# Raw sums of x kept in DRAM, and the down weights' GpSimd work dealt out by units

## The chip, the cores and the metric

The kernel runs on one core of one Trainium2 chip. The metric is device time in microseconds from start to end of one execution, lower is better. Where several executions of a kernel were timed, their median stands for it.

The engines are named as the profile names them: PE is TensorE (matmuls), PEld its weight loads, DVE is VectorE, ACT is ScalarE, POOL is GpSimd, SP is SyncE, which here only issues DMA. Every engine runs its own instructions in program order and waits for the others by semaphores. A DMA that an engine issues waits in that engine's order too, so an issue that cannot go yet holds everything that is queued behind it on this engine.

## The reference

For one sequence of S = 2048 tokens of width D = 576, all in float32:

```python
g = sigmoid((x * gate_w).sum(-1, keepdims=True))
a = linear_attention(x, wqkv, wo)      # 32 heads of 18; phi(t) = max(t, 0) + exp(min(t, 0)) + 1e-6
b = (gelu(x @ w_gate) * (x @ w_up)) @ w_down     # inner width 4608
out = g * a + (1 - g) * b
```

The attention is linear: per head a matrix of phi(k) and v and a sum of phi(k) are made over all tokens, and each query's row is multiplied by the matrix and divided by its product with the sum.

## The kernel before

**Split operands.** PE multiplies numbers of a reduced float32 type. Each operand is therefore split into a high part (an ACT or POOL copy into that type) and a low part (raw minus high, on DVE or POOL), and a product is high times high, plus high times low, plus low times high. The contraction of 576 rows is halved into 288 and 288 and each half kept as three row tiles (kt = 0, 1, 2); the third has 32 rows and carries its low part inside the same tile, so a slot of x has five parts: three high, two low.

**Fast 2x2 products.** The three feed-forward products are computed on 2x2 blocks with seven instead of eight block products (`SEQUENCE`, `PRODUCTS`, lines 32 to 35). Their operands are the blocks A11, A12, A22 of x and the sums S1 to S4 of blocks, and for the weights B11, B21, B22 and T1 to T4. The order of the seven is written out by hand.

**Stages in time.** Tokens come in four blocks of 512, which form two pairs (p = 0, 1) for the feed-forward.

1. Keys, gate and the state sums (to about 145 us in the profile).
2. Queries, denominators and the mix (about 145 to 317 us): for each block `query` makes phi(q) in five head groups (lines 420 to 431), `halves_of` splits it on ACT and DVE (`hl`, lines 557 and 558), `den` makes the denominators on PE (line 567). `reciprocals` (lines 626 to 643) inverts them on DVE in two halves per block (line 632), and spreads each to all head rows by a store to DRAM (line 633, `rden_d`) and a load from it (line 637, `rb`), both on SP. `scaled` multiplies phi(q) by it on DVE (line 649) and splits the result into `p` (ACT line 65, DVE line 66). `mixed` multiplies p by the output matrix on PE (line 668) and ACT stores the gated result (line 673). The order of all these calls is written out by hand (lines 688 to 784).
   In the same stage the sums S1 to S4 of the *second* pair's x are made ahead. They come in six pieces (three row tiles, two column halves): `ahead_load` on SP (line 387), `ahead_make` on POOL (four sums by `sum_blocks`, lines 377 to 380, then four casts, line 395, and four subtracts, line 398), and `ahead_store` on SP (lines 405 and 406) of the high and low parts to DRAM (`xop_d`). `next_ahead(k)` stores piece k-1, loads piece k+1 and makes piece k. Two buffers hold pieces, one holds high parts. The first pair's sums come from whole row tiles (`Chunk`), summed on DVE and split by ACT (line 607) and POOL (line 610). At the end of the stage ACT issues the load of the ready gate weights (line 766) into the place where the pieces stood.
3. Gate and up (about 317 to 1131 us): 72 chains, each seven block products of seven matmuls for one pair p, one block column n and one of gate or up (`CHAINS`, `gu_steps`, matmuls in line 806). Eight PSUM banks turn over between PE and its readers. For gate, DVE combines the products and ACT applies the gelu; for up, DVE combines and multiplies, makes the sums of h and stores h to DRAM by SP (line 837). `w_fetch` and `w_split` (lines 810 to 821) load, sum on POOL and split the next weights. The first chains are all of pair 0: chains 0 to 3 are (p 0, n 0) and (p 0, n 1), chains 4 and 5 (p 1, n 1). So the second pair's seven x slots (`X[1]`, tile `xo2`), loaded from `xop_d` in chains 0 to 3 (`XO2_AT`, line 995), are first used in chain 4. The results of pair 0 lie in the tiles `e0` and `e123`, those of pair 1 in `ES[1]`, four tiles `f0` to `f3`.
4. Down (about 1131 us to the end): six groups s of inner rows, each with two pairs p and seven products k, 84 units (`unit`, matmuls in line 1045, 36 to a unit). `h_load` and `h_make` (lines 969, 974 ACT, 975 DVE) bring back and split h three or more units ahead. DVE adds each product into an accumulator in SBUF (line 1053), which starts from the gated attention result (`acc_load`, line 1022). A bank that a later product adds to must have been read by DVE first. `d_fetch` (line 951) loads a group's four down weight blocks; `d_make` (lines 953 to 961) copies one operand on ACT (line 956), makes its low part on POOL in two halves (line 958) and, after B11, makes T1, T2 and T3 in six POOL halves (line 961), after B21 T4 in two. The next group's fetch goes after unit (p 0, k 4), its first two operands after unit (p 1, k 0), then one to a unit.

Of the kernel before, what the change touches and what calls it, by code (L numbers as in the profile page):

```python
# [8 lines left out]
F32 = mybir.dt.float32  # L9
F32R = mybir.dt.float32r  # L10
AF = mybir.ActivationFunctionType
OP = mybir.AluOpType
# [26 lines left out]
def tile_gated_mix(ctx, tc, xt, xs, xn, wk, wv, wq, wo, wgu, wdn, cst, out):  # L39
# [7 lines left out]
    rden_d = {(b, h): dram.tile([7 * NG, BS // 2], F32, name=f"rden_d{b}{h}") for b in range(NB) for h in range(2)}  # L47
    xop_d = dram.tile([128, 7, 5, BS], F32, name="xop_d")
    ga_d = [dram.tile([128, D], F32, name=f"ga_d{i}") for i in range(NST)]
# [334 lines left out]
    def ahead_load(k):  # L384
        kt, c = k // 2, slice(k % 2 * 256, k % 2 * 256 + 256)
        raw = xup.tile([128, 4, 256], F32, name="xu")
        nc.sync.dma_start(raw, xs[1, kt, :, :, c])
        ahead[k] = [raw]

    def ahead_make(k):  # L390
        kt, (raw,) = k // 2, ahead[k]
        sum_blocks(raw, nc.gpsimd)
        hi = xup.tile([128, 4, 256], F32R, name="xuh", bufs=1)
        for i in range(4):
            nc.gpsimd.tensor_copy(hi[:, i], raw[:, i])
            o = raw[:, i].bitcast(F32R) if kt < 2 else hi[32:64, i]
            p = slice(0, 128) if kt < 2 else slice(32, 64)
            nc.gpsimd.tensor_tensor(o, raw[p, i], f32(hi[p, i]), OP.subtract)
        ahead[k] = [hi, raw]

    def ahead_store(k):
        kt, c = k // 2, slice(k % 2 * 256, k % 2 * 256 + 256)
        hi, lo = ahead.pop(k)
        if kt < 2:
            nc.sync.dma_start(xop_d[:, S2:S1 + 1, 3 + kt, c], lo)
# [186 lines left out]
    aheads = Scope()  # L592
    xup = aheads.pool("xup", bufs=2, side="right")
    for k in range(2):
# [97 lines left out]
    query(0, 0)  # L692
    ahead_make(0)
    query(0, 1)
# [255 lines left out]
    def d_fetch(s):  # L950
        nc.sync.dma_start(draw[:, :4], wdn[ORDER[s]].rearrange("p i g c -> p i (g c)"))

    def d_make(s, k):
        b = PRODUCTS[SEQUENCE[k]][1]
        w, src = wd[(7 * s + k) % 8], draw[:, DAT[b]]
        nc.scalar.activation(w[:, 0], src, AF.Copy)  # L956
        for c in (slice(0, 432), slice(432, 864)):
            nc.gpsimd.tensor_tensor(w[:, 1, c], src[:, c], f32(w[:, 0, c]), OP.subtract)  # L958
        for o, x, y in {B11: ((D11, D12, D11), (DX, D22, D11), (D12, D22, D12)), B21: ((D21, D21, DX),)}.get(b, ()):
            for c in (slice(0, 432), slice(432, 864)):  # L960
                nc.gpsimd.tensor_tensor(draw[:, o, c], draw[:, x, c], draw[:, y, c], OP.subtract)  # L961

# [21 lines left out]
    for c, chain in enumerate(CHAINS):  # L984
        for i, step in enumerate(first_steps if c == 0 else gu_steps(*chain)):
            if c or i >= EARLY:
                step()
            if i == 0 and c in at:
                n, m = at[c]
                w_split(m)  # L990
                if (n, m) != (NF2 - 1, 1):
                    w_fetch(n + m, 1 - m)
            for k in XO2_AT.get((c, i), ()):
                a = PRODUCTS[SEQUENCE[k]][0]
# [143 lines left out]
```

## Time and profile before

| | before |
|---|---|
| median of three executions | 1547.41 us (1545.75 to 1548.58) |
| the profiled execution | 1559.55 us |
| its span, first to last instruction | 1557.8 us |
| PE busy | 1511.2 us, 97% |
| DVE, ACT, POOL busy | 65%, 35%, 47% |
| mean clock granted to PE | 0.986 |
| bytes moved by DMA | 248.19 MB, mean 159 GB/s |

The profiled execution is one run with the hardware profiler on; all stamps and durations come from it, and it is 12.1 us longer than the median. "<-" names what ended an engine's wait, as semaphore events show it. Lines are those of the kernel before. In timelines a row is start, duration, engine, line, operation, output and inputs, count, and in brackets the wait before it; rows of SPq and ACTq are DMA issues. In groups the number after the count is total busy time and mean ns of one, then the idle time before them.

### The profile page before, as it was taken

How to read it: one execution, taken by the hardware profiler on the slowest of the kernel's cores; microseconds unless marked ns; L12 is line 12 of the kernel's file. 1: busy time of each engine (PE TensorE's matmuls, PEld its weight loads, DVE VectorE, ACT ScalarE, POOL GpSimd, SP SyncE). 2: the span in 40 equal slices, each digit the busy share in tenths (PEclk: the TensorE clock that was granted, in tenths of full speed). 3: DMA queues.
4: the chain of work that ended last, by engine and by line, in shares of the span. 5: the costliest groups of instructions: out<-in, count | busy, mean ns of one | idle time of the engine just before them, and what ended most of it. 6: DMA issues, size and time to landing. Idle time of an engine off the chain costs nothing.

```text
span 1557.8 us, 21591 instructions
## 1 busy us (share of the span) xinstructions
PE 1511.2 (97%) x8354; PEld 1333.0 (86%) x8354; DVE 1005.9 (65%) x1314; ACT 539.3 (35%) x703; POOL 735.6 (47%) x560
## 2 busy tenths in 40 slices
PE   8999987999999999999999999999999979999999
PEld 8998876887888888888888888888799979999999
DVE  7886765456655566665556666555776676758675
ACT  6554533432223222222322222232234333534431
POOL 3653468165455445445544544552528050725530
PEclk9999988999999999999999999999999989999999
DMA  7553364684323233322223332223795635556574
GB/s 241 151 166 107 131 216 160 214 307 180 111 95 109 97 134 135 135 104 100 105 99 135 135 135 102 101 102 139 269 331 208 208 121 206 168 179 193 184 218 141
DMA packets 99310, 248.19 MB, mean 159 GB/s; under 512 B 8960, under 2 KB 38296, under 8 KB 96264
## 3 DMA queue, kind: packets, MB, share of 16 engines
q1 hardware_dynamic: 96184, 234.96, 43.7%
q10 hardware_dynamic: 3024, 11.86, 2.1%
q8 instruction: 65, 1.06, 0.3%
q14 instruction: 37, 0.30, 0.1%
HBM read 157.24 MB, written 89.55 MB: 158 GB/s over the span
## 4 chain that ended last, share of the span: by engine, by line
PE 75%; issue 2%; DVE 2%; POOL 1%; ACT 1%; DMA 1%; SPq 0%; ACTq 0%; DVEq 0%
PE bank L806 51%; PE bank L1045 22%; PE pair L668 2%; POOL stage L961 1%; POOL wd L958 0%; DMA acc<-ga_d 0%; ACT xo L974 0%; DVE f L834 0%; DVE acc L1053 0%; DMA ga_d<-ga 0%; DMA xop_d<-xuh 0%; ACT wd L956 0%; DVE u L844 0%; ACT ga L673 0%; POOL xo L958 0%
## 5 line engine op out<-in xcount | busy, mean ns | idle before, releaser
L806 PE MATMUL bank<-xo,wu 128*128 128x512 f32 x1764 | 413.3, 394 | 1.5 <-ACT p L850 1.3
L806 PE MATMUL bank<-xo,wg 128*128 128x512 f32 x1764 | 413.4, 394 | 1.2 <-ACT ga L673 0.8
L806 PEld LDWEIGHTS bank<-xo,wu 128*128 128x128 f32 x1764 | 332.4, 189 | 79.2 <-ACT p L850 1.8
L806 PEld LDWEIGHTS bank<-xo,wg 128*128 128x128 f32 x1764 | 332.2, 189 | 78.5 <-ACT ga L673 1.1
L814 POOL TENSOR_TENSOR stage<-stage 128x384 f32<-128x384 f32 x136 | 159.5, 1192 | 45.7 <-DMA stage<-wgu 43.0
L1053 DVE SCALAR_TENSOR_TENSOR acc<-bank,gate,acc 128x288 f32<-128x288 f32 x288 | 137.0, 509 | 58.5 <-PE bank L1045 51.3
L820 POOL TENSOR_TENSOR wg<-stage,wg 128x768 fp32r<-128x768 f32 (+1 forms) x34 | 72.2, 2125 | 190.1 <-ACT wg L819 188.8
L850 ACT ACTIVATE p<-bank 128x512 f32<-128x512 f32 x72 | 43.0, 597 | 343.9 <-PE bank L806 343.9
L820 POOL TENSOR_TENSOR wu<-stage,wu 128x768 fp32r<-128x768 f32 (+1 forms) x34 | 79.8, 2346 | 146.1 <-ACT wu L819 144.8
L1045 PE MATMUL bank<-xo 128*128 128x288 f32 x1044 | 143.6, 297 | 5.1 <-DVE acc L1053 3.8
L1045 PEld LDWEIGHTS bank<-xo 128*128 128x128 f32 x1044 | 141.0, 190 | 6.1 <-DVE acc L1053 4.3
L958 POOL TENSOR_TENSOR wd<-stage,wd 128x432 fp32r<-128x432 f32 x40 | 61.8, 1570 | 155.2 <-ACT wd L956 155.2
L855 DVE TENSOR_TENSOR u<-bank,p 128x512 f32<-128x512 f32 x72 | 49.5, 687 | 94.8 <-PE bank L806 92.2
L1045 PE MATMUL bank<-wd,xo 128*128 128x288 f32 x792 | 107.7, 297 | 1.2 <-DVE acc L1053 1.2
L1045 PEld LDWEIGHTS bank<-wd,xo 128*128 128x128 f32 x792 | 106.4, 190 | 1.5 <-DVE acc L1053 1.5
L958 POOL TENSOR_TENSOR xo<-stage,xo 128x432 fp32r<-128x432 f32 x44 | 64.2, 1486 | 79.3 <-ACT xo L956 79.2
L841 DVE TENSOR_TENSOR e<-bank,u 128x512 f32<-128x512 f32 x54 | 37.2, 691 | 79.7 <-PE bank L806 76.9
L841 DVE TENSOR_TENSOR f<-bank,u 128x512 f32<-128x512 f32 x54 | 37.2, 691 | 76.1 <-PE bank L806 76.0
L831 ACT ACTIVATE f<-f 128x512 f32<-128x512 f32 x54 | 34.1, 632 | 140.8 <-DVE f L841 140.8
L668 PE MATMUL pair<-kw,p 126*128 126x288 f32 (+1 forms) x480 | 71.7, 311 | 9.8 <-ACT p L65 9.7
L668 PEld LDWEIGHTS pair<-kw,p 126*128 126x128 f32 (+1 forms) x480 | 70.9, 204 | 11.6 <-ACT p L65 10.2
L869 DVE TENSOR_TENSOR u<-bank,u 128x512 f32<-128x512 f32 x72 | 49.8, 692 | 38.4 <-PE bank L806 36.4
(189 smaller groups left out, 2314.7 us busy)
## 6 DMA issues: line engine op xcount, KB each, us to landing
h_d<-sx SPq DMA_DIRECT2D x108, 256.0 KB
stage<-wgu SPq DMA_DIRECT2D x34, 768.0 KB
xo<-h_d SPq DMA_DIRECT2D x29, 768.0 KB
e<-h_d SPq DMA_DIRECT2D x28, 768.0 KB
hraw<-h_d SPq DMA_DIRECT2D x27, 768.0 KB
h_d<-e SPq DMA_DIRECT2D x72, 256.0 KB
h_d<-f SPq DMA_DIRECT2D x72, 256.0 KB
stage<-wdn SPq DMA_DIRECT2D x6, 1728.0 KB
```

The costliest lines, as they stand in the source:

```text
L668: nc.tensor.matmul(y[:, i, :288], p[:R, a, g], KW[g][:R, wl, i * 288:(i + 1) * 288], start=(n == 0), stop=(n == 14))
L806: nc.tensor.matmul(ps, w_, x_, start=start and i == 0, stop=i == 6, skip_group_check=not start)
L814: nc.gpsimd.tensor_tensor(o, a, b, OP.subtract)
L820: nc.gpsimd.tensor_tensor(w[:, i, 3:5], src[:, :, 0:2], f32(w[:, i, 0:2]), OP.subtract)
L831: nc.scalar.activation(es[i], es[i], AF.Gelu_apprx_tanh)
L841: nc.vector.tensor_tensor(es[i], a, b, OP.add)
L850: nc.scalar.activation(p1, ps["a"], AF.Copy)
L855: nc.vector.tensor_tensor(u2, b, p1, OP.add)
L869: nc.vector.tensor_tensor(u3, c, u2, OP.add)
L958: nc.gpsimd.tensor_tensor(w[:, 1, c], src[:, c], f32(w[:, 0, c]), OP.subtract)
L1045: nc.tensor.matmul(y, h[:, hl, g, t * 128:(t + 1) * 128], w[:, wl, g * 288:(g + 1) * 288], start=k in (1, 5) and n == 0, stop=n == len(ops ...
L1053: nc.vector.scalar_tensor_tensor(o, y, gate[:, 1, st:st + 1], o, op0=OP.mult, op1=OP.add)
```

## The change

Part one: the sums of the second pair are no longer split ahead. POOL makes the four sums of a piece, and SP stores the raw piece (`xsum_d`) as one contiguous block. There are three piece buffers, no high buffer, and the load of the piece after next now stands ahead of the store of the last one. `xop_d` keeps the three unsummed blocks. The raw sums are loaded into the second pair's result tile `f` (one tile of four blocks now), two blocks to a piece, and split in chains 1 to 3: high on ACT, low on DVE for the first two row tiles and on POOL for the third.

Part two: the sums T1 to T4 of the down weights become tasks of their own (`d_sum`), and splits and sums are dealt out one to a unit; the last two operands of a group are split after its own first two units. The fetch goes one unit earlier (after k 3). In the last three gate and up chains the first group's tasks are spread in the same way. The accumulator loads of the second pair go to units 4 to 7 instead of 2 to 5.

```diff
-    xop_d = dram.tile([128, 7, 5, BS], F32, name="xop_d")
+    xop_d = dram.tile([128, 3, 5, BS], F32, name="xop_d")
+    xsum_d = [dram.tile([128, 4, 256], F32, name=f"xsum_d{k}") for k in range(6)]
...
-    def ahead_make(k):
-        kt, (raw,) = k // 2, ahead[k]
-        sum_blocks(raw, nc.gpsimd)
-        hi = xup.tile([128, 4, 256], F32R, name="xuh", bufs=1)
-        for i in range(4):
-            nc.gpsimd.tensor_copy(hi[:, i], raw[:, i])
-            o = raw[:, i].bitcast(F32R) if kt < 2 else hi[32:64, i]
-            p = slice(0, 128) if kt < 2 else slice(32, 64)
-            nc.gpsimd.tensor_tensor(o, raw[p, i], f32(hi[p, i]), OP.subtract)
-        ahead[k] = [hi, raw]
+    def ahead_sums(k):
+        sum_blocks(ahead[k], nc.gpsimd)
 
     def ahead_store(k):
-        kt, c = k // 2, slice(k % 2 * 256, k % 2 * 256 + 256)
-        hi, lo = ahead.pop(k)
-        if kt < 2:
-            nc.sync.dma_start(xop_d[:, S2:S1 + 1, 3 + kt, c], lo)
-        nc.sync.dma_start(xop_d[:, S2:S1 + 1, kt, c], f32(hi))
+        nc.sync.dma_start(xsum_d[k], ahead.pop(k))
 
     def next_ahead(k):
-        ahead_store(k - 1)
-        if k < 5:
+        if 0 < k < 5:
             ahead_load(k + 1)
-        ahead_make(k)
+        if k:
+            ahead_store(k - 1)
+        ahead_sums(k)
...
-    xup = aheads.pool("xup", bufs=2, side="right")
+    xup = aheads.pool("xup", bufs=3, side="right")
...
-    ahead_make(0)
+    next_ahead(0)
...
-    ES[1] = [bothp.tile([128, BS], F32, name=f"f{i}") for i in range(4)]
+    f = bothp.tile([128, 4, BS], F32, name="f")
+    ES[1] = [f[:, i] for i in range(4)]
...
-        for o, x, y in {B11: ((D11, D12, D11), (DX, D22, D11), (D12, D22, D12)), B21: ((D21, D21, DX),)}.get(b, ()):
-            for c in (slice(0, 432), slice(432, 864)):
-                nc.gpsimd.tensor_tensor(draw[:, o, c], draw[:, x, c], draw[:, y, c], OP.subtract)
+
+    def d_sum(t):
+        o, x, y = {T1: (D11, D12, D11), T2: (DX, D22, D11), T3: (D12, D22, D12), T4: (D21, D21, DX)}[t]
+        for c in HALVES:
+            nc.gpsimd.tensor_tensor(draw[:, o, c], draw[:, x, c], draw[:, y, c], OP.subtract)
...
-    XO2_AT = {(0, 4): (0, 1), (1, 1): (2,), (1, 4): (3,), (2, 1): (4,), (2, 4): (5,), (3, 1): (6,)}
+    X_AT = {(0, 5): A11, (2, 2): A12, (3, 2): A22}
+    S_AT = [(1, 1), (1, 4), (2, 1), (2, 4), (3, 1), (3, 4)]
+
+    def s_raw(k):
+        return f[:, k % 2 * 2:k % 2 * 2 + 2].rearrange("p a (b c) -> p (a b) c", b=2)
+
+    def s_load(k):
+        if k < 6:
+            nc.sync.dma_start(s_raw(k), xsum_d[k])
+
+    def s_make(k):
+        kt, c, raw = k // 2, slice(k % 2 * 256, k % 2 * 256 + 256), s_raw(k)
+        rows, lo, eng = (slice(0, 128), 3 + kt, nc.vector) if kt < 2 else (slice(32, 64), kt, nc.gpsimd)
+        nc.scalar.activation(X[1][:, S2:S1 + 1, kt, c], raw, AF.Copy)
+        eng.tensor_tensor(X[1][rows, S2:S1 + 1, lo, c], raw[rows], f32(X[1][rows, S2:S1 + 1, kt, c]), OP.subtract)
+
+    for k in range(2):
+        s_load(k)
     LAST = len(CHAINS) - 1
+    D_AT = {(LAST - 2, 0): lambda: d_make(0, 0), (LAST - 2, 4): lambda: d_sum(T1), (LAST - 1, 0): lambda: d_sum(T2),
+            (LAST - 1, 2): lambda: d_make(0, 1), (LAST - 1, 4): lambda: d_make(0, 2), (LAST - 1, 6): lambda: d_sum(T3),
+            (LAST, 1): lambda: d_make(0, 3), (LAST, 4): lambda: d_sum(T4)}
...
+            if (c, i) in S_AT:
+                k = S_AT.index((c, i))
+                s_make(k)
+                s_load(k + 2)
...
-                d_make(0, 0)
-            if c == LAST - 1 and i in (1, 3, 5):
-                d_make(0, (i + 1) // 2)
+            if (c, i) in D_AT:
+                D_AT[c, i]()
...
-        if 2 <= u < 6:
-            acc_load(1, 2 * u - 4)
-            acc_load(1, 2 * u - 3)
+        if 4 <= u < 8:
+            acc_load(1, 2 * u - 8)
+            acc_load(1, 2 * u - 7)
...
-            if p == 0 and k == 4:
+            at = 7 * p + k
+            if at == 3:
                 d_fetch(s + 1)
-            if p == 1 and k == 0:
-                d_make(s + 1, 0)
-            if p == 1 and k < 6:
-                d_make(s + 1, k + 1)
+            elif at in (5, 8, 9, 11, 13):
+                d_make(s + 1, (5, 8, 9, 11, 13).index(at))
+            elif at in (6, 7, 10, 12):
+                d_sum((T1, T2, T3, T4)[(6, 7, 10, 12).index(at)])
+        if s and p == 0 and k < 2:
+            d_make(s, 5 + k)
```

More of the change, by code (lines that the diff above doesn't have):

```diff
@@ L384, in ahead_load @@
     def ahead_load(k):
-        kt, c = k // 2, slice(k % 2 * 256, k % 2 * 256 + 256)
-        raw = xup.tile([128, 4, 256], F32, name="xu")
-        nc.sync.dma_start(raw, xs[1, kt, :, :, c])
-        ahead[k] = [raw]
-    def ahead_make(k):
-        kt, (raw,) = k // 2, ahead[k]
-        sum_blocks(raw, nc.gpsimd)
-        hi = xup.tile([128, 4, 256], F32R, name="xuh", bufs=1)
-        for i in range(4):
-            nc.gpsimd.tensor_copy(hi[:, i], raw[:, i])
-            o = raw[:, i].bitcast(F32R) if kt < 2 else hi[32:64, i]
-            p = slice(0, 128) if kt < 2 else slice(32, 64)
-            nc.gpsimd.tensor_tensor(o, raw[p, i], f32(hi[p, i]), OP.subtract)
-        ahead[k] = [hi, raw]
-    def ahead_store(k):
-        kt, c = k // 2, slice(k % 2 * 256, k % 2 * 256 + 256)
-        hi, lo = ahead.pop(k)
-        if kt < 2:
-            nc.sync.dma_start(xop_d[:, S2:S1 + 1, 3 + kt, c], lo)
-        nc.sync.dma_start(xop_d[:, S2:S1 + 1, kt, c], f32(hi))
+        raw = ahead[k] = xup.tile([128, 4, 256], F32, name="xu")
+        nc.sync.dma_start(raw, xs[1, k // 2, :, :, k % 2 * 256:k % 2 * 256 + 256])
+    def ahead_sums(k):
+        sum_blocks(ahead[k], nc.gpsimd)
+    def ahead_store(k):
+        nc.sync.dma_start(xsum_d[k], ahead.pop(k))
     def next_ahead(k):
-        ahead_store(k - 1)
-        if k < 5:
+        if 0 < k < 5:
             ahead_load(k + 1)
-        ahead_make(k)
+        if k:
+            ahead_store(k - 1)
+        ahead_sums(k)
     def wv_make(kt):
@@ L951, in d_fetch @@
         nc.sync.dma_start(draw[:, :4], wdn[ORDER[s]].rearrange("p i g c -> p i (g c)"))
+    HALVES = slice(0, 432), slice(432, 864)
     def d_make(s, k):
[L954 to L955 removed]
+        w, src = wd[(7 * s + k) % 8], draw[:, DAT[PRODUCTS[SEQUENCE[k]][1]]]
         nc.scalar.activation(w[:, 0], src, AF.Copy)
[L957 removed]
+        for c in HALVES:
             nc.gpsimd.tensor_tensor(w[:, 1, c], src[:, c], f32(w[:, 0, c]), OP.subtract)
[L959 to L961 removed]
+    def d_sum(t):
+        o, x, y = {T1: (D11, D12, D11), T2: (DX, D22, D11), T3: (D12, D22, D12), T4: (D21, D21, DX)}[t]
+        for c in HALVES:
+            nc.gpsimd.tensor_tensor(draw[:, o, c], draw[:, x, c], draw[:, y, c], OP.subtract)
     def raw_of_h(j):
@@ L992, in tile_gated_mix @@
                     w_fetch(n + m, 1 - m)
-            for k in XO2_AT.get((c, i), ()):
-                a = PRODUCTS[SEQUENCE[k]][0]
+            if (c, i) in X_AT:
+                a = X_AT[c, i]
                 nc.sync.dma_start(f32(X[1][:, a]), xop_d[:, a])
+            if (c, i) in S_AT:
+                k = S_AT.index((c, i))
+                s_make(k)
+                s_load(k + 2)
             if i == 0 and c == LAST - 3:
```

## The prediction

> **What bounds the kernel now.** I read the page's engine shares first (PE busy 97%), then PE's waits, a table by stage, and the timelines around each long wait. PE's waits (total us, times, longest):
>
> ```profile
> PE bank L1045 <- DVE acc L1053: 15.0, 5, 8.7
> PE pair L668 <- ACT p L65: 9.7, 1, 9.7
> PE den L567 <- ACT hl L557: 8.4, 2, 6.2
> PE bank L806 <- ACT p L850: 1.3, 1, 1.3
> ```
>
> The first is the down stage, the next two the query and mix stage, the last the seam between gate/up and down. Two stretches of 100 us (window, length, busy time and count of PE, PEld, DVE, ACT, POOL, granted clock, DMA share, GB/s):
>
> ```profile
> 200.00:300.00 100.00, 80.42 (x455) 72.03 (x454) 55.67 (x65) 37.02 (x54) 62.94 (x68) 0.86 0.55 186
> 400.00:500.00 100.00, 100.00 (x433) 81.28 (x432) 59.26 (x78) 28.78 (x37) 50.87 (x35) 1.00 0.30 107
> ```
>
> In gate/up PE never rests. In the mix stage it rests 19.6 us, and the clock granted to it is 0.86:
>
> ```profile
> 228.86 0.80 PE L567 MATMUL den<-hl,zmk 126*128 126x512 f32 x1 [6.23 <-ACT hl L557]
> 230.77 0.79 PE L567 MATMUL den<-hl,zmk 126*128 126x512 f32 x1 [1.11 <-DVE hl L558]
> 231.36 5.71 PE L668 MATMUL pair<-kw,p 126*128 126x288 f32 x30
> 240.65 4.13 PE L668 MATMUL pair<-kw,p 126*128 126x288 f32 x30
> ...
> 268.02 6.21 PE L668 MATMUL pair<-kw,p 126*128 126x288 f32 x30 [9.73 <-ACT p L65]
> 276.40 1.73 PE L567 MATMUL den<-hl,zmk 72*128 72x512 f32 x2 [2.16 <-ACT hl L557]
> 277.93 10.25 PE L668 MATMUL pair<-kw,p 126*128 126x288 f32 x60
> ```
>
> **Part 1: pieces of x kept unsplit.** Why PE rests there: SP's queue, then DVE.
>
> ```profile
> 202.43 0.62 SPq L387 DMA_DIRECT2D xu<-xs  x1
> 211.54 0.36 SPq L405 DMA_DIRECT2D xop_d<-xu  x1
> 215.46 0.59 SPq L387 DMA_DIRECT2D xu<-xs  x1
> 216.15 0.86 SPq L633 DMA_DIRECT2D rden_d<-rb  x2
> 219.86 1.72 SPq L637 DMA_DIRECT2D rb<-rden_d  x2
> 256.42 0.90 SPq L633 DMA_DIRECT2D rden_d<-rb  x2
> 259.19 1.72 SPq L637 DMA_DIRECT2D rb<-rden_d  x2
> ```
> ```profile
> 200.43 1.75 DVE L632 RECIPROCAL rb<-rb 35x256 f32<-35x256 f32 x1
> 218.78 0.69 DVE L431 SCALAR_TENSOR_TENSOR r<-bank,r 126x512 f32<-126x512 f32 x1 [0.24 <-ACT r L430]
> 226.46 1.05 DVE L649 SCALAR_TENSOR_TENSOR r<-r,rb 126x640 f32<-126x640 f32 x1 [6.99 <-DMA rb<-rden_d]
> 246.72 1.75 DVE L632 RECIPROCAL rb<-rb 35x256 f32<-35x256 f32 x1
> 266.38 0.83 DVE L649 SCALAR_TENSOR_TENSOR r<-r,rb 126x640 f32<-126x640 f32 x1 [11.02 <-DMA rb<-rden_d]
> ```
>
> Block 3's reciprocals are ready at 202.2 (200.43 + 1.75) and leave at 216.15. Ahead of them in SP's queue stand piece 1's store, which waits for POOL's split (211.54), and piece 3's load, which waits until that store frees one of two buffers (215.46). Block 0's are ready at 248.5 and leave at 256.42; ahead of them the program has piece 4's store, which waits for the same split. The scaling on DVE then waits 6.99 and 11.02, behind it ACT's p and hl, and last PE. POOL's split:
>
> ```profile
> L395 POOL CAST xuh<-xu 128x256 fp32r<-128x256 f32 x24 | 19.4, 808 | 21.8 <-DMA xop_d<-xuh 21.4
> L398 POOL TENSOR_TENSOR xu<-xu,xuh 128x256 fp32r<-128x256 f32 x16 | 14.6, 914 | 1.3
> ```
>
> The change takes out these 40 instructions and eight narrow ones, over 34.0 us of POOL, and the 21.4 us that POOL waited for the one high buffer, and four of ten 512 KB stores. SP's store then waits for four sums only. The load, now ahead of the store, waits for the store before that; for piece 3 that is piece 0's, which had freed its buffer by 202.43 even with twice the bytes. So block 3's reciprocals leave at about 203, are loaded 3.7 later (216.15 to 219.86) and are there 6.6 after that (to 226.46): 213.3, while DVE's turn comes at 219.47 (218.78 + 0.69). With 6 us to spare the waits of 6.23 and 1.11 go, and the cold mix (5.71 for 4.13) with them: 8.9. DVE's chain moves up by only 7.0 (226.46 to 219.47), so the den after it is about 1.0 late: **7.9**, bounds 0 (SP held as now) and 8.9.
>
> PE then reaches block 0's first mix at 250.4 (268.02 − 9.73 − 7.9). Block 0's reciprocals are ready at 240.6 (248.5 − 7.9) and leave at once; the loads go 2.8 later (256.42 to 259.19), the first lands 7.2 after (to 266.38) at 250.6, and 0.83 of scaling and 0.8 of ACT's p make 252.2. Of 9.73 I leave 1.5 (the first half can leave before the second is made), bounds 0 and 4. The 2.16 comes from ACT's issue of the gate weights' load, held by the last piece's store:
>
> ```profile
> 273.95 0.74 ACT L673 ACTIVATE ga<-pair,gate 128x576 f32<-128x576 f32 x1 [5.98 <-DMA xop_d<-xuh]
> ```
>
> Sums alone let that store out earlier, so it goes. The cold mixes give 2.08 (6.21 for 4.13) and 1.99 (10.25 for 8.26). 9.73 + 2.16 + 2.08 + 1.99 − 1.5, less 1.0 for what is late next (block 1's reciprocals take as long as before under shorter mixes): **13.5**.
>
> Here the Trainium skill (TensorE: Matmul & The Clock Gate, Part 1) gives another price for the clock: after an idle window of some 3.4 us the array runs at half rate for about as long, which would be an estimated 1.7 for each gap over 3.4. By it the cold work behind 6.23, 9.73 and the down stage's 8.66 is 5.1, where the rows here and below give 8.7 with a gap of 2.57; the sum would be about 3.6 smaller.
>
> The splitting moves to chains 1 to 3: six copies of 128x1024 on ACT, four subtracts of 128x1024 on DVE, two of 32x1024 on POOL. The nearest row:
>
> ```profile
> L975 DVE TENSOR_TENSOR xo<-e,xo 128x1536 fp32r<-128x1536 f32 x17 | 32.0, 1883 | 8.8 <-ACT xo L974 8.8
> ```
>
> Two thirds of that is 1.3 on each of DVE's, 5.2 in all, beside 40% of idle time (59.26 busy in the window above) and with eight PSUM banks between PE and DVE; ACT is 29% and POOL 51% busy there. The loads fall from 8,960 to 6,912 KB, but PE waited for none of them. The loads of A11, A12 and A22 go up to a chain later with the same bytes; they are first used in chain 4. New waits: a split on ACT for its piece's load, with the gelu queued behind it; its subtract on DVE for ACT, with the bank reads behind it, for which PE waits; and on SP the load of the piece after next for that subtract, with the weight fetch and h stores behind it. A chain is 11.3 us (49 matmuls at 433 to 100), so a piece's load has half a chain or more from issue to use, over 5 us. I take **−0.5**, bounds 0 and −5.2 (all of DVE's exposed).
>
> **Part 2: down weights one task to a unit.** In each group ACT's second weight copy waits for six POOL instructions (L961), and the down input's split queues behind it on ACT, then DVE, then PE:
>
> ```profile
> 1246.04 6.50 POOL L961 TENSOR_TENSOR stage<-stage 128x432 f32<-128x432 f32 x6
> ```
> ```profile
> 1250.41 0.93 ACT L956 ACTIVATE wd<-stage 128x864 fp32r<-128x864 f32 x1 [6.61 <-POOL stage L961]
> ```
> ```profile
> 1252.74 9.89 DVE L975 TENSOR_TENSOR xo<-hraw,xo 128x1536 fp32r<-128x1536 f32 x1 [7.28 <-ACT xo L974]
> 1331.13 2.50 DVE L975 TENSOR_TENSOR wu<-e,wu 128x1536 fp32r<-128x1536 f32 x1 [7.25 <-ACT wu L974]
> ```
> ```profile
> 1185.88 3.61 PE L1045 MATMUL bank<-xo 128*128 128x288 f32 x18 [2.57 <-DVE acc L1053]
> 1263.12 4.69 PE L1045 MATMUL bank<-xo,wu 128*128 128x288 f32 x18 [8.66 <-DVE acc L1053]
> 1334.12 2.64 PE L1045 MATMUL bank<-xo,wg 128*128 128x288 f32 x18 [1.25 <-DVE acc L1053]
> 1336.59 4.94 PE L1045 MATMUL bank<-xo,wu 128*128 128x288 f32 x36
> ```
>
> After the change a unit (4.8 us) holds one split or one sum of two halves, a third of 6.50, 2.2 us; T2 is made a unit before its copy, T3 and T1 likewise. So the five waits go: 15.0, and cold matmuls of 2.05 (4.69 for 2.64) and 0.97 (3.61 for 2.64). The fetch comes one unit earlier and its first user two, leaving 9.5 us instead of 14.3. The first fetch, among the accumulator loads:
>
> ```profile
> 1161.56 0.59 SPq L951 DMA_DIRECT2D stage<-wdn  x1
> ```
> ```profile
> 1173.06 0.93 ACT L956 ACTIVATE wd<-stage 128x864 fp32r<-128x864 f32 x1 [1.26 <-DMA stage<-wdn]
> ```
>
> It took 11.5. ACT will stand at that copy, the next down input's split behind it; DVE needs that split half a unit later, so 9.5 + 2.4 − 0.93 = 11 are free and more is paid. Moving the other accumulator loads behind this fetch helps it. I charge 2.0 at the first group (0 to 4), nothing at the others, where no such loads run: 15.0 + 3.0 − 2.0 = **16.0**. Copies 5 and 6 go to the next group's first two units, five ahead of their use; the accumulator loads to units 4 to 7, three or more ahead of theirs; I cost both at nothing, with some 14 us of cover. In the seam a weight copy leaves ACT's path to p L850: **1.0** of the 1.3 (0 to 1.3).
>
> **Sum.** 7.9 + 13.5 − 0.5 + 16.0 + 1.0 = 37.9 off the profiled 1559.55 (span 1557.8, 1.75 around it): 1521.6. That execution stands 12.1 above the median of 1547.41. 9.5 of it looks like its own: DVE's 9.89, where its sister took 2.50, made 8.66 of a wait that elsewhere is 1.25, 7.4, and 2.05 of cold matmuls. If so, 28.4 are to be had in an ordinary run: **1519.0**. If every run has it, 1509.5.
>
> **Rivals.**
> - *SP is held anyway.* The load ahead of the store waits for a store to land; piece 0's landed only at 202.43. If block 0's reciprocals stay behind it, the 13.5 stays: 1532.5. Against it, twice the bytes were in the way.
> - *The fetch is late in every group*, at 2 to 4 each in four more: 1527 to 1535. For it 11.5 against 11; against it, the later fetches share the queue with less.
> - *DVE is starved by POOL.* The 9.89 lay wholly under POOL's work. If the four new subtracts, each reading two SBUF tensors beside POOL's weight split, are held 7.4 longer, 30 more fall on DVE in chains 1 to 3 (34 us, some 14 idle): about 15 exposed, 1534. Beside it stands the Trainium skill (GPSIMD Engine Reference, 8. Key points): GpSimd shares its SBUF interfaces with VectorE, and contends with instructions of two SBUF inputs; that agrees with 2.50 against L975's 1883 ns mean, and speaks against this change.
> - *Slower: f becomes one tile.* If waits went by tile and not by block, each of eight writes to f per column block would wait for the h store in flight.
>
> ```profile
> L841 DVE TENSOR_TENSOR e<-bank,u 128x512 f32<-128x512 f32 x54 | 37.2, 691 | 79.7 <-PE bank L806 76.9 <-DMA h_d<-e 2.7
> ```
>
> A block column is four chains of 49 matmuls, 45.3 us at 433 to 100; DVE works 59.26% of it and has 18.4 idle. Eight waits of w lose 8w − 18.4 in each of 18 columns: more than the gain from w = 2.5 on. The one wait seen was 2.7: 3.2 x 18 = 58, so 1577. Against it, e's blocks 1 to 3 are one tile now, and 54 instructions met that wait once.
> - *It doesn't do what it says.* Another wait of the same length stands behind each (the reciprocals' load takes 6 to 7 us by itself): about 1547. Against it are the 6 us to spare.
>
> **How the numbers follow.** My forecast of 1519 has a chance of 0.58; the same course with 9.5 more to gain (1509.5) 0.14; SP held 0.09; fetch late 0.06; DVE starved 0.04; f 0.05; no effect 0.04. The range of 1505 to 1534 takes in the first three and the starved case, and part of the late fetch; f, no effect and the tail of the rest, under 0.2, are out. About 0.2% (3 us) is what a measurement of this kernel can tell from no change. Faster is 0.58 + 0.14 + 0.09 + 0.06 + 0.04 = 0.91, same 0.04, slower 0.05.
>
> **What would show it.** Right: L633 leaves right behind L632; no PE wait over 2 us between 200 and 300; PE's wait for DVE acc L1053 under 5 us in all; no ACT weight copy (L956 before) that waits for POOL for 6 us; chains 1 to 6 as long as before. Wrong: PE still waits 6 us or more for p or hl; PE waits in chains 1 to 4 for DVE or for x's operands; ACT waits over 2 us for the down weights' fetch in group after group; or PE's rests go and the clock stays down.

## The result and the profile after

The changed kernel takes 1523.9 us (median of four executions, 1522.54 to 1526.23), the kernel before on the same chip 1547.82 (four, 1545.75 to 1548.58): a ratio of 0.9849, 95% interval 0.9832 to 0.9866. I had forecast 1519.0, within 1505 to 1534. The profiled execution of the changed kernel takes 1522.8, its span is 1521.0, so 36.8 less than the span before; by the prediction's sum it was 37.9 less.

The first view is again PE's waits, of the changed kernel (total us, times, longest). L794 is L806 of before, L555 L567, L656 L668, L1060 L1045.

```profile
PE bank L794 <- DVE e L829: 6.0, 2, 5.6
PE den L555 <- DVE hl L546: 2.6, 4, 1.3
...
PE pair L656 <- ACT p L66: 1.0, 1, 1.0
...
PE bank L1060 <- DVE acc L1068: 0.4, 1, 0.4
```

The three long waits of before (15.0, 9.7, 8.4) are gone. A new one heads the list: gate/up, which never rested, now waits 5.6 at one place. The windows show it too (columns as in the prediction): the mix stage is up from 80.42 to 95.43 busy at a clock of 0.98, and the stretch behind it has lost 6.

```profile
200.00:300.00 100.00, 95.43 (x585) 86.05 (x584) 59.77 (x71) 44.23 (x64) 37.72 (x32) 0.98 0.61 222
300.00:400.00 100.00, 93.96 (x394) 75.61 (x393) 66.39 (x72) 32.30 (x40) 65.01 (x41) 0.97 0.41 149
```

For an account by stage, PE's timeline gives three marks: the first mix behind 190, the rest of chain 0 behind the last mix, and the first down product. First before, then after:

```profile
192.05 4.27 PE L668 MATMUL pair<-kw,p 126*128 126x288 f32 x30
...
315.62 5.10 PE L806 MATMUL bank<-xo,wg 128*128 128x512 f32 x21 [0.83 <-ACT ga L673]
...
1130.96 3.90 PE L1045 MATMUL bank<-xo 128*128 128x288 f32 x27
```
```profile
190.32 4.26 PE L656 MATMUL pair<-kw,p 126*128 126x288 f32 x30
...
292.48 5.10 PE L794 MATMUL bank<-xo,wg 128*128 128x512 f32 x21 [0.83 <-ACT ga L661]
...
1114.21 3.93 PE L1060 MATMUL bank<-xo 128*128 128x288 f32 x27
```

| stretch | before | after | gained | predicted |
|---|---|---|---|---|
| start to the first mix | 192.05 | 190.32 | 1.7 | 0 |
| mix | 123.57 | 102.16 | 21.4 | 7.9 + 13.5 = 21.4 |
| gate and up, with the seam | 815.34 | 821.73 | −6.4 | −0.5 + 1.0 |
| down (to the span's end) | 426.84 | 406.79 | 20.05 | 16.0 |

So the two terms of the mix came out as worked in their sum, the down term was too small, and the splitting in the chains had the wrong size. The 1.7 of the start is no gain of the change: the profiles of two runs below begin the first mix at 190.19 (b2, the kernel before) and 191.49 (after2, the changed kernel). The down stage varies as well: 423.4 to 426.8 in the six profiles that keep its old schedule, 406.8 and 407.1 in two of the changed kernel.

### The profile page after: what moved, and what is told of

It reads as the page before. It is cut to its first block, busy times and chain, and to the rows that moved or that the text cites. A ratio compares the mean times of both kernels' runs of the same rounds, so it can differ in the third digit from the quotient of the medians.

```text
span 1521.0 us, 21582 instructions
## 1 busy us (share of the span) xinstructions
PE 1500.8 (99%) x8354; PEld 1323.7 (87%) x8354; DVE 1011.2 (66%) x1318; ACT 545.5 (36%) x709; POOL 721.1 (47%) x514
## 4 chain that ended last, share of the span: by engine, by line
PE 74%; DVE 2%; DMA 2%; issue 1%; SPq 0%; ACT 0%; DVEq 0%; ACTq 0%
PE bank L794 49%; PE bank L1060 24%; DMA h_d<-f 1%; DMA stage<-wdn 1%; DVE f L822 0%; DMA acc<-ga_d 0%; DVE xo L967 0%; SPq L1037 0%; DVE u L832 0%; DVE sx L871 0%; DVE sx L872 0%; DVE f L873 0%; DVE acc L1068 0%; ACT xo L966 0%; ACT wu L966 0%
## 5 line engine op out<-in xcount | busy, mean ns | idle before, releaser
L794 PE MATMUL bank<-xo,wg 128*128 128x512 f32 x1764 | 415.1, 395 | 6.9 <-DVE e L829 6.0
L794 PE MATMUL bank<-xo,wu 128*128 128x512 f32 x1764 | 413.8, 395 | 0.0
L794 PEld LDWEIGHTS bank<-xo,wg 128*128 128x128 f32 x1764 | 333.1, 189 | 84.7 <-DVE e L829 6.9
L794 PEld LDWEIGHTS bank<-xo,wu 128*128 128x128 f32 x1764 | 333.4, 189 | 77.5 <-DMA wu<-wp_d 0.3
L1060 PE MATMUL bank<-xo 128*128 128x288 f32 x1044 | 141.8, 295 | 1.7 <-DVE u L832 1.3
L1060 PEld LDWEIGHTS bank<-xo 128*128 128x128 f32 x1044 | 139.4, 188 | 2.4 <-DVE u L832 1.6
L1060 PE MATMUL bank<-wd,xo 128*128 128x288 f32 x792 | 106.8, 296 | 0.0
L1060 PEld LDWEIGHTS bank<-wd,xo 128*128 128x128 f32 x792 | 105.6, 188 | 0.0
L829 DVE TENSOR_TENSOR f<-bank,u 128x512 f32<-128x512 f32 x54 | 37.3, 692 | 76.9 <-PE bank L794 76.0
L829 DVE TENSOR_TENSOR e<-bank,u 128x512 f32<-128x512 f32 x54 | 37.2, 691 | 77.0 <-PE bank L794 76.8
L953 POOL TENSOR_TENSOR stage<-stage 128x432 f32<-128x432 f32 x48 | 76.3, 1616 | 0.0
L819 ACT ACTIVATE e<-e 128x512 f32<-128x512 f32 x54 | 34.1, 632 | 97.2 <-DVE e L829 97.2
```

What stands on the lines that cost most here:

```text
L794: nc.tensor.matmul(ps, w_, x_, start=start and i == 0, stop=i == 6, skip_group_check=not start)
L819: nc.scalar.activation(es[i], es[i], AF.Gelu_apprx_tanh)
L829: nc.vector.tensor_tensor(es[i], a, b, OP.add)
L1060: nc.tensor.matmul(y, h[:, hl, g, t * 128:(t + 1) * 128], w[:, wl, g * 288:(g + 1) * 288], start=k in (1, 5) and n == 0, stop=n == len(ops ...
```

## The experiments

The kernel before stood at two levels, for the most part by chip: 1547.8 (first chip) and 1547.83 (17 executions, the last test's chip), and 1558.34 (11), 1558.09 (15) and 1557.11 (17; 1545.74 to 1568.87) on the chips of the others. Both levels also occur on one chip: 1 of the 11 (1547.99) and 5 of the second 17 (1545.74 to 1550.19) lie at the lower one, at a mean granted clock of 0.991 to 0.992 where the others there have 0.986 to 0.989. Differences are therefore given against the kernel before of the same chip.

**One part alone.** The first kernel has part one and the old down stage, the second the old pieces of x and part two:

```diff
  # p1, from the changed kernel (d_fetch, d_make and the unit loop are those of before)
-            if (c, i) in D_AT:
-                D_AT[c, i]()
+            if c == LAST - 1 and i in (1, 3, 5):
+                d_make(0, (i + 1) // 2)
...
  # p2, from the kernel before (d_make, d_sum and the unit loop are those of the change)
-            if c == LAST - 1 and i in (1, 3, 5):
-                d_make(0, (i + 1) // 2)
+            if (c, i) in D_AT:
+                D_AT[c, i]()
```

> Part 1 alone (pieces of x unsplit, down stage as before). My theory, from the two profiles: the mix stage loses 21.4 us, gate/up gains about 8 (PE's wait of 5.6 for DVE e, 0.4 more, and the cold matmuls behind it), the down stage keeps its five waits: 1547.8 - 13.4 = 1534.4, and the profile shows the wait of 5 to 6 in the third chain. Rival: the wait in the third chain belongs to the two parts together; then it is absent here and the time is about 1527.

> Part 2 alone (down weights one task to a unit, x split ahead as before). My theory: the seam loses 1.5, the down stage the four short waits and their cold matmuls, about 10.6, since the 9.5 of the profile of before was that execution's own: 1547.8 - 12.1 = 1535.7. Rival: every run of before has the long stall in the down stage; then part 2 takes off about 20 and the time is 1526. The mix stage shows its waits of 6.2, 9.7 and 2.2 as before.

Part one alone: 1542.77 (1540.13 to 1544.52) against 1558.34, ratio 0.9905 (0.9883 to 0.9927), 15.6 gained. Part two alone: 1538.34, ratio 0.9879 (0.9857 to 0.9901), 20.0 gained. PE's waits, p1 and then p2 (here L1055 is the down product):

```profile
PE bank L1055 <- DVE acc L1063: 14.4, 5, 8.7
PE bank L794 <- DVE e L829: 6.0, 2, 5.6
```
```profile
PE den L567 <- ACT hl L557: 11.0, 2, 7.1
PE pair L668 <- ACT p L65: 7.5, 1, 7.5
```

The parts are independent: the new wait of 5.6 comes with part one alone, the old ones of the mix stay with part two alone, and 15.6 + 20.0 is 35.6, near the 36.8 of the two profiles. Part one gives less than the 21 or so that I had for it; what is missing is of the size of the new wait. Part two gives more than the 17. So part one came near its theory (13.4), and part two gave what its rival had (20), not the 12.1 of the theory; the kernel before stands 10.5 higher on this chip than the 1547.8 from which both were reckoned.

**The same kernel on the other level.** The unaltered changed kernel, and the kernel before once more with a profile:

> The changed kernel unaltered, beside the kernel before on one chip, to give the ratio where the kernel before takes about 1558. Theory (the 9.89 us split belongs to the kernel before whenever its POOL tasks stand as they do, and the changed kernel has none): 1521 to 1525, so some 34 less than before there. Rival (whatever makes the kernel before 10 us longer here lies in the chip and adds to every kernel): about 1533.

> The kernel before, profiled once more. My theory: DVE's 9.89 us split and PE's wait of 8.66 in the down stage were that execution's own; here the same split takes about 2.5, the wait is about 1.25, and the profiled time is 1547 to 1550. Rival: they belong to the kernel and come again, with a profiled time near 1559.

The changed kernel took 1522.93 (1522.46 to 1524.38) where the kernel before took 1558.09: ratio 0.9779 (0.9766 to 0.9793), 35.2 gained instead of 23.9. Its own time hardly differs between the chips (1523.9); the kernel before differs by 10. On this level the gain is near the whole sum of 37.9, with no 9.5 taken off. The second profile of before took 1554.36 and has the same wait of 8.7. DVE's timeline there:

```profile
1248.30 9.89 DVE L975 TENSOR_TENSOR xo<-hraw,xo 128x1536 fp32r<-128x1536 f32 x1 [7.28 <-ACT xo L974]
```

The same instruction, the same transition between groups, the same 9.89. It is not "that execution's own", as I had it.

**What holds that split.** Two kernels keep the schedule of before and move addresses only: one exchanges two places of the split down input, the other allocates the raw tile of h first.

```diff
- hb = ([h_view(xf[:, 6912 + i * 3072:...]) for i in range(3)] +
+ hb = ([h_view(xf[:, 6912 + i * 3072:...]) for i in (1, 0, 2)] +      # hperm
...
+ hraw.append(dp.tile([128, 3, BS], F32, name="hraw"))                 # hraddr: ahead of acc
  acc = [dp.tile([128, 4, 4, 288], F32, name=f"acc{p}") for p in range(NP)]
...
- hraw.append(dp.tile([128, 3, BS], F32, name="hraw"))
```

> The kernel before with the first two of the five places of the split down input exchanged (its order xo1, xo0, xo2, wg, wu); the schedule is the same to the instruction. If DVE's 9.89 us split hangs on which addresses DVE and POOL touch, it goes or moves to another unit, the longest wait of PE for the accumulator falls from 8.7 to 1 to 3, and the time falls from 1558 to about 1548. Rival (it hangs on when DVE starts against POOL's run of instructions): the same 9.9 at the same unit, and 1558.

> The kernel before with the third raw tile of h taken from the pool first instead of last, so that it, the accumulators and the weight tiles lie at other addresses; the schedule is the same. If DVE's split of 9.89 hangs on where this tile lies, it goes (2.5 at that unit, PE's longest wait for the accumulator 1 to 3) and the time falls from 1558 to about 1548. Rival (it hangs on the instructions' timing alone): 9.9 again, 1558.

Times: 1557.38 against 1558.09, ratio 1.0007 (0.9989 to 1.0024), and 1557.47 against 1557.11, ratio 1.002 (0.999 to 1.0049). DVE's timelines, hperm and hraddr:

```profile
1251.66 9.89 DVE L975 TENSOR_TENSOR xo<-hraw,xo 128x1536 fp32r<-128x1536 f32 x1 [7.28 <-ACT xo L974]
```
```profile
1249.95 9.89 DVE L975 TENSOR_TENSOR xo<-hraw,xo 128x1536 fp32r<-128x1536 f32 x1 [7.28 <-ACT xo L974]
```

Neither change of address removed it, and both expectations of 1548 fell. (POOL's tile `stage` lay where it was in both.) POOL's timeline of hperm shows what lies beside it:

```profile
1251.42 2.20 POOL L958 TENSOR_TENSOR wd<-stage,wd 128x432 fp32r<-128x432 f32 x2
...
1257.79 2.14 POOL L958 TENSOR_TENSOR xo<-stage,xo 128x432 fp32r<-128x432 f32 x2
```

DVE's split starts 0.24 behind POOL's first, POOL runs on without a break, two instructions in 2.14 to 2.20 (1.07 each), until 1259.93, and DVE ends 1.62 after that (1251.66 + 9.89 = 1261.55). A split takes about 1.75 alone, so by these stamps DVE got nothing done while POOL had work, over eight instructions of POOL.

**One call earlier.** This kernel is before with the first weight copy of a group, and POOL's six sums, a unit earlier:

```diff
- if p == 1 and k == 0:
+ if p == 0 and k == 6:
      d_make(s + 1, 0)
```

> The kernel before with one call moved: the first weight copy of the next group, and with it POOL's six halves of sums, one unit earlier (after unit p 0, k 6 instead of p 1, k 0); nothing is dealt out to units. Theory (the waits of the down stage come from ACT's second weight copy standing 6.6 for the six halves, with the down input's split behind it): a unit is 4.8, so that copy waits 2 or less, PE's waits for the accumulator fall from 15 to 1 to 4 in all, the 9.89 goes, since DVE's split no longer comes late, and 13 to 19 are gained. Rival (POOL's run of ten and more instructions itself holds DVE, whenever it comes): splits of 2.5 to 9.9 still lie beside it, PE waits 5 to 10, and under 10 are gained. In both the first group may lose 2 to 4 to its fetch.

1543.05 (1540.92 to 1547.03, 12 executions) against 1547.83, ratio 0.9967 (0.9956 to 0.9978), 4.8 gained. In time that is what the rival expected, but the profile is the theory's. First PE's waits, then DVE and POOL at the same transition, POOL's two instructions there one by one (shortest, median and longest in ns), and PE's first down product:

```profile
PE pair L668 <- ACT p L65: 12.0, 2, 7.8
PE den L567 <- ACT hl L557: 9.8, 2, 6.0
PE bank L1045 <- ACT bank L1049: 1.8, 1, 1.8
...
PE bank L1045 <- DVE acc L1053: 0.9, 1, 0.9
```
```profile
1250.81 2.49 DVE L975 TENSOR_TENSOR xo<-hraw,xo 128x1536 fp32r<-128x1536 f32 x1 [2.40 <-ACT xo L974]
```
```profile
1250.56 3.73 POOL L958 TENSOR_TENSOR wd<-stage,wd 128x432 fp32r<-128x432 f32 x2
```
```profile
L958 POOL TENSOR_TENSOR wd<-stage,wd x2: 1132/1890/2647, 1250.6 to 1251.6; 128x432 fp32r<-128x432 f32 x2
```
```profile
1135.07 3.92 PE L1045 MATMUL bank<-xo 128*128 128x288 f32 x27
```

In the down stage the theory holds: the waits are 0.9 and 1.8, 2.7 in all, the split takes 2.49, though it starts the same 0.25 behind POOL, and the stage takes 409.5 (1544.6 − 1135.07) instead of 426.84, 17.3 less. Most of part two's 20.05 is this one call. POOL's two instructions beside the split did not slow alike: the first took 1.13, no longer than beside the held split (1.11 to 1.12 in hperm), the second 2.65. By the stamps the two engines took turns: POOL's first ends at 1251.69, DVE's split 1.61 behind it at 1253.30, and POOL's second 0.99 behind that.

But this execution lost 4 ahead of the down stage, which the edit doesn't touch (1135.07 against 1130.96): the waits of the mix stage are 12.0 and 9.8 where the first profile has 9.7 and 8.4. And the kernel before of this chip stands at 1547.83. If the 8.7 and its cold matmuls, 9.5 in all, are not in those executions, 17.3 − 9.5 − 4 = 4 is to be expected, near the 4.8; with them it would be 13. The agreement is loose, since the old down stage varies by 3.4 between profiles and this profile stands 3.3 above its kernel's median. So the two levels fit the held split being there or not, and the clock fits too: part two alone, which has the mix of before and no held split, has the 0.991 to 0.993 of the lower level. That is inferred: no profile of the kernel before at the lower level was taken.

**The new wait.** In the changed kernel, three of DVE's four subtracts and the read behind them, POOL's weight split beside each, and PE:

```profile
303.30 1.70 DVE L983 TENSOR_TENSOR xo<-f,xo 128x1024 fp32r<-128x1024 f32 x1 [1.70 <-ACT xo L982]
...
308.33 1.71 DVE L983 TENSOR_TENSOR xo<-f,xo 128x1024 fp32r<-128x1024 f32 x1
...
319.94 2.76 DVE L983 TENSOR_TENSOR xo<-f,xo 128x1024 fp32r<-128x1024 f32 x1
...
323.39 0.69 DVE L829 TENSOR_TENSOR e<-bank,u 128x512 f32<-128x512 f32 x1
```
```profile
302.90 1.02 POOL L809 TENSOR_TENSOR wg<-stage,wg 32x384 fp32r<-32x384 f32 x1
...
307.34 1.62 POOL L809 TENSOR_TENSOR wg<-stage,wg 32x512 fp32r<-32x512 f32 x1
...
318.94 2.67 POOL L808 TENSOR_TENSOR wu<-stage,wu 128x1024 fp32r<-128x1024 f32 x1
```
```profile
324.13 3.35 PE L794 MATMUL bank<-xo,wg 128*128 128x512 f32 x7 [5.58 <-DVE e L829]
327.28 12.48 PE L794 MATMUL bank<-xo,wu 128*128 128x512 f32 x49
```

PE's last product of chain 2, the seventh, adds to the bank of the fourth (`s3` and `s5`), and so needs the read of that one (L829), which ends at 324.08 behind three subtracts and the 1.70 that DVE waited for ACT. Each subtract ends 1.1 behind the end of the POOL instruction that was running when it began: 305.00 behind 303.92, 310.04 behind 308.96, 322.70 behind 321.61. Two kernels take this apart. One places the first four splits elsewhere, the other leaves POOL's low parts of the next block's weights out.

```diff
- S_AT = [(1, 1), (1, 4), (2, 1), (2, 4), (3, 1), (3, 4)]
+ S_AT = [(0, 5), (0, 6), (2, 4), (2, 6), (3, 1), (3, 4)]      # smove
...
- w_split(m)
+ w_split(m, n > 1)      # nolow: no low parts for n = 1
```

> The changed kernel with the six splits at other steps: two in the first chain, where DVE has nothing to do, two behind the fourth product of the third, the last two as they were. My theory: PE waited in the third chain because the reader of one bank on DVE (the fourth product's, whose bank the seventh adds to) was queued behind three subtracts that ran 1.7 to 2.8 us beside POOL; ahead of that reader stands none now, so the wait of 5.6 and the cold matmuls go: 1516, with under 1 us of PE wait in chains 1 to 4. Rival 1: DVE is slowed by POOL wherever the subtracts stand; the wait moves to the fourth chain and 1521 to 1524 results. Rival 2: the pieces' loads are late in the first chain, ACT waits for them with the gelu behind: 1518 to 1522.

> The changed kernel; it leaves out the low parts of the second column block's weights (two of four POOL instructions of two weight splits, 8 narrow and wide subtracts in chains 1 to 4). Theory (the new subtracts take 1.7 to 2.8 instead of 1.3 because POOL's weight work runs beside them): those beside the hole fall to 1.3 to 1.4, PE's wait of 5.6 for the bank's reader falls to under 2, time 1516 to 1520. Rival (the wait comes from the subtracts' place in DVE's queue whatever their length): the wait stays at 4 to 5.6 and the time at 1522 to 1524.

smove takes 1517.51 (1515.32 to 1519.07) against 1558.34, ratio 0.9747 (0.9724 to 0.977); nolow 1514.4 (1512.8 to 1516.2) against 1558.09, ratio 0.9723 (0.971 to 0.9736). In both the wait of 5.6 for L829 is gone. DVE's subtracts in smove and in nolow (there L985):

```profile
296.56 1.23 DVE L983 TENSOR_TENSOR xo<-f,xo 128x1024 fp32r<-128x1024 f32 x1 [1.65 <-ACT xo L982]
...
319.32 2.93 DVE L983 TENSOR_TENSOR xo<-f,xo 128x1024 fp32r<-128x1024 f32 x1 [3.18 <-ACT xo L982]
```
```profile
301.41 1.23 DVE L985 TENSOR_TENSOR xo<-f,xo 128x1024 fp32r<-128x1024 f32 x1 [1.69 <-ACT xo L984]
...
314.07 1.22 DVE L985 TENSOR_TENSOR xo<-f,xo 128x1024 fp32r<-128x1024 f32 x1
```

With POOL idle beside it the subtract takes 1.23, as I had priced it (1.3); beside POOL's weight work 1.4 to 2.9 in these three kernels. Without that work the same places cost no wait, and 8.5 are gained over the changed kernel on the same chip (1522.93). So both are causes: the place in DVE's queue, and POOL. POOL's share is more than the new subtracts: the three take 6.17 in the changed kernel and 3.88 in nolow, and five sums and products of h ahead of the read (L871 to L883 in the changed kernel) 7.28 and 4.15. smove is the fastest kernel of this study that leaves no work out, 5.4 to 6.4 under the two medians of the changed kernel, which were taken on other chips. It is not free of POOL: its third subtract takes 2.93, and PE waits 0.8 and 1.0 for POOL's weights instead, where under 1 in all was expected.

**The mix stage.** Two kernels ask what the gain there hung on. The first is before with the third and the last piece called behind the reciprocals; the second is the changed kernel with two buffers and the store ahead of the load.

```diff
-    next_ahead(2)                        # swap
     reciprocals(3)
+    next_ahead(2)
...
-    next_ahead(5)
     den(0, 4)
     reciprocals(0)
+    next_ahead(5)
...
-    xup = aheads.pool("xup", bufs=3, side="right")      # twobuf
+    xup = aheads.pool("xup", bufs=2, side="right")
...
         if k:
             ahead_store(k - 1)
+        if 0 < k < 5:
+            ahead_load(k + 1)
```

> The kernel before with the order of its calls alone altered: the third and the last piece's store, load and split are called behind the next reciprocals instead of ahead of them, so that the stores of the reciprocals stand ahead in the queue of SP; POOL's work, the bytes and the splits stay. Theory (SP's order alone made the gaps of 6.23 and 9.73): both fall under 2, 15 to 20 less than before. Rival (POOL's 34 us and its SBUF traffic slow DVE or ACT as well): waits of 3 to 6 stay, 5 to 12 less.

> The changed kernel with two piece buffers instead of three and each piece's store ahead of the next load in the queue of SP, as before; POOL still makes sums only. Theory (the gaps of the mix stage came from POOL's 34 us of splitting ahead of the stores): no wait of PE over 2.6 comes back there, 1521 to 1525. Rival (the third buffer and the order of load and store removed them): waits of 5 to 10 for p or hl come back, 1535 to 1545.

swap is slower than before: 1564.33 (1562.75 to 1566.68) against 1558.09, ratio 1.0045 (1.0031 to 1.0058). Its PE, and its SP and ACT:

```profile
258.16 2.38 PE L567 MATMUL den<-hl,zmk 126*128 126x512 f32 x4 [6.23 <-ACT hl L557]
268.99 6.18 PE L668 MATMUL pair<-kw,p 126*128 126x288 f32 x30 [8.46 <-ACT p L65]
```
```profile
205.66 0.67 SPq L633 DMA_DIRECT2D rden_d<-rb  x2
...
252.90 0.55 SPq L387 DMA_DIRECT2D xu<-xs  x1
...
254.21 0.67 SPq L633 DMA_DIRECT2D rden_d<-rb  x2
```
```profile
257.48 1.15 ACT L557 ACTIVATE hl<-r 126x512 fp32r<-126x512 f32 x2 [11.67 <-DMA xu<-xs]
```

Block 3's reciprocals leave at 205.66 and the wait of 6.23 that PE had at 228.86 is gone: that half of the theory holds. Block 0's are still held, by the call for the fifth piece, which I had left in place (its load, at 252.90, waits for the store behind POOL's split). So the wait only moved to 258, where ACT has stood 11.67, by the profile for that same load. `hl` doesn't read what that load brings; why ACT stood is open. A third wait, of 8.00, follows at 283. Both expectations missed; this order doesn't empty the queue while POOL needs 34 us for the splits.

twobuf takes 1531.15 (1526.11 to 1534.01) against 1557.11, ratio 0.9824 (0.9775 to 0.9874). In its profile:

```profile
226.25 1.74 PE L555 MATMUL den<-hl,zmk 126*128 126x512 f32 x2 [3.20 <-ACT hl L545]
260.65 0.49 PE L555 MATMUL den<-hl,zmk 72*128 72x512 f32 x1 [2.04 <-ACT hl L545]
300.77 5.09 PE L794 MATMUL bank<-xo,wg 128*128 128x512 f32 x21 [0.83 <-ACT ga L661]
```

It begins the mix at 192.47 and so needs 108.3 for the stage, between the 102.16 of the changed kernel and the 123.57 of before. Neither expectation holds: some 15 of the 21.4 come from POOL making sums only, with its fewer bytes, and some 6 from the third buffer and the order.

**The accumulator loads.** The changed kernel with the second pair's loads at units 2 to 5 again:

```diff
- if 4 <= u < 8:
-     acc_load(1, 2 * u - 8)
+ if 2 <= u < 6:
+     acc_load(1, 2 * u - 4)
```

> The changed kernel with the second pair's accumulator loads back at units 2 to 5, so around the first fetch of down weights as before. Theory (moving them behind the fetch is what made the 2.0 that I charged come out at 0.35): the fetch lands later, ACT's wait for it grows from 6.6 to 8 or more, PE waits 1 to 3 there, 1523 to 1526. Rival (the fetch's two units of lead cover it anyway): PE's wait stays under 0.5, 1522 to 1524.

1529.35 (1525.73 to 1531.48) against 1557.11, ratio 0.9817 (0.9776 to 0.9859). ACT and PE, first in the changed kernel, then here:

```profile
1148.40 0.93 ACT L946 ACTIVATE wd<-stage 128x864 fp32r<-128x864 f32 x1 [6.59 <-DMA stage<-wdn]
```
```profile
1152.67 0.93 ACT L946 ACTIVATE wd<-stage 128x864 fp32r<-128x864 f32 x1 [9.49 <-DMA stage<-wdn]
```
```profile
1157.93 2.18 PE L1060 MATMUL bank<-xo 128*128 128x288 f32 x9 [3.63 <-DVE acc L1068]
```

ACT waits 2.9 longer for the fetch, and PE 3.63 at the place where the changed kernel waits 0.4. The mechanism is the theory's, but it costs more than expected: 3.63 where I had 1 to 3, and 1529.35 where I had 1523 to 1526. The down stage takes 413.0 instead of 406.8.

## Why the prediction was right, and where it was off

- **Mix, 7.9 + 13.5.** Right in sum: 21.4 of 21.4. Up to the mix at 240.65 before (230.41 in the changed kernel) 8.5 of it are gained, behind it 12.9, so each term is near its share. First SP's rows of the changed kernel, then DVE's:

```profile
203.33 1.47 SPq L621 DMA_DIRECT2D rden_d<-rb  x2
...
237.32 2.33 SPq L621 DMA_DIRECT2D rden_d<-rb  x2
```
```profile
198.69 1.75 DVE L620 RECIPROCAL rb<-rb 35x256 f32<-35x256 f32 x1
...
237.61 1.75 DVE L620 RECIPROCAL rb<-rb 35x256 f32<-35x256 f32 x1
```

  Block 3's reciprocals are ready at 200.4 and leave at 203.33, where I had "about 203"; block 0's first half leaves at 237.32, before the second is made (237.61 + 1.75). The waits left are 2.6 for `hl` and 1.0 for `p`, where I had left 1.0 + 1.5 + 1.0. That the load waits "for the store before that", and so needs its third buffer, is what twobuf shows, at a price of 6.
- **Splitting, "I take −0.5, bounds 0 and −5.2".** This step failed, in size and in its cover: the stretch lost 6.4 although the seam's wait of 1.3 for L850 went, so the splits cost 7.7, beyond my bounds. The "eight PSUM banks" were no cover, because the last product needs the bank of the fourth, three places ahead of it. "PE waits in chains 1 to 4 for DVE", one of my signs of being wrong, came. In the kernel before, DVE's read and PE's chain at that place:

```profile
339.91 0.69 DVE L841 TENSOR_TENSOR e<-bank,u 128x512 f32<-128x512 f32 x1
```
```profile
331.86 11.46 PE L806 MATMUL bank<-xo,wg 128*128 128x512 f32 x49
```

  The read ends at 340.6, and the last seven of 49 matmuls begin at about 341.7 (331.86 + 42/49 of 11.46): a slack of 1.1. Ahead of that read the change put three subtracts of 1.70, 1.71 and 2.76 and a wait for ACT of 1.70 into DVE's queue. The idle 40% of DVE is a mean. And my price of 1.3 was that of a subtract alone; the rival "DVE is starved by POOL" named the mechanism, but it came as 0.4 to 1.5 on each subtract and not as 7.4. In smove the same stretch takes 814.89, so the splits themselves need cost no more than 0.9 (815.34 less the seam's 1.3 is 814.04).
- **Clock.** Behind the gap of 5.58, seven matmuls took 3.35, where seven take 1.78, and the next 49 took 12.48, where 49 take 11.46: 1.6 and 1.0 too much, 2.6 in all. The granted clock is 0.50 over the first 3.15 us and 0.70 over the next 3.72. The rule that I had weighed (the Trainium skill, TensorE: Matmul & The Clock Gate, Part 1) gives an estimated 1.7; this row speaks for the dearer price.
- **Down, "15.0 + 3.0 − 2.0".** Right in kind: no accumulator wait over 0.4 is left. The 2.0 of the first fetch came to 0.35, because the accumulator loads stand behind it (accearly: 3.63 without that). The other 2 or so lie in no single wait that I can name; the old stage's spread between profiles, 3.4, can hold them. The rival "fetch late in every group" fell as a cost: PE waits at most 0.4. But its sign came: ACT stands 6.59, 7.37, 7.10, 6.83 and 5.79 for the fetch in the five groups (L946), while PE hardly waits.
- **The other rivals.** SP didn't hold block 0, and `f` as one tile brought no wait for the h stores (DVE's idle time before L829 on `f` is 76.9, and 76.0 of it ends on PE).
- **The median, "9.5 of it looks like its own".** The number served, the reason fell: the held split is in all six profiles that keep the old down schedule (before, b2, hperm, hraddr, swap, p1) and in no other. The gain is 23.9 where I had 28.4, so 4.5 short. By stages it is 1.2 short (7.2 too much for the splitting, less 0.3, 4.0 and 1.7 of more gain at the seam, in the down stage and at the start). That is partly luck: the one large error was made up by the start and by the down stage, where the kernel's profiles differ among themselves. The other 3.3 are the distance to the medians: the profiled execution of before stands 11.7 above its median and that of after 1.1 below, 12.8 in all, where I had taken off 9.5.

## What to carry to other kernels

Before work is moved beside a chain of accumulating products, look at how early each bank's reader ends before that bank is needed again, not at the engine's mean idle time; the slack here was 1.1 us under 40% idle. Price an instruction that reads two SBUF tensors on DVE by a row that lies beside the same POOL work; here it waited for the end of POOL's running instruction and then took its own time. Before a long task of POOL ahead of a store is sped up or reordered, count the issues that queue behind that store: removing the work and adding a buffer helped, moving two of the calls did not.

## What the runs showed of the hardware

A DVE subtract of two SBUF tensors beside running POOL subtracts went in two ways. Mostly the engines took turns, instruction by instruction: at the transition in early DVE needs 2.49 instead of 1.75, and of POOL's two one takes 1.13 and the next 2.65; in the changed kernel the three new subtracts ahead of the late read end 1.1 behind the end of POOL's running instruction. At one transition, in six profiles, POOL ran on at 1.07 and DVE stood until POOL had nothing left, 9.89. The Trainium skill (GPSIMD Engine Reference, 8. Key points) has such instructions contend; these rows agree, and show two prices. What decides between them isn't settled: the offset of DVE to POOL (0.24 and 0.25) is the same in both, and two changes of address left it as it was.
